# Loading the first x tile ahead of a small weight, and rearranging the other start-up loads, in a two-layer attention and GLU kernel

## The chip, the cores and the metric

The kernel runs on one core of one Trainium2 chip. The metric is device time in microseconds (us). The granted TensorE clock, where it is on record, is 0.999 to 1.00 in all but four executions, where it is 0.996. Before the change: 391.91 us, median of 3 runs (391.82 to 392.07).

## The reference

Two linear-attention blocks alternate with two gated MLP blocks over x of shape 1 x 2048 x 512 in bf16. Cut to what matters here:

```python
def _A_ref(x, wqkv, w_phi, wo):               # 32 heads of 16
    q, k, v = split(x @ wqkv)
    pq, pk = q @ w_phi, k @ w_phi             # per head, 16 x 16
    phi_q = concat(softmax(pq), softmax(-pq)) # 32 features a head
    phi_k = concat(softmax(pk), softmax(-pk))
    kv, z = phi_k^T v, sum(phi_k)             # sums over all 2048 rows
    return ((phi_q kv) / (phi_q z + 1e-6)) @ wo
def _B_ref(x, W_gate, W_up, W_down):
    return (relu(x W_gate) * (x W_up)) @ W_down
x = x + _A_ref(layernorm(x)); x = x + _B_ref(layernorm(x))   # and both once more
```

`kv` sums over all rows, so no query of the first block can be finished before the keys of all 16 tiles of 128 rows are normalised and summed. I call the time up to there the first phase.

## The kernel before

The kernel records about 3,700 operations, each with an estimated duration, and a list scheduler inside the kernel file puts them in an order for each engine (SyncE's queue of DMAs included). It tries many orders and keeps the one that its own model finds shortest.

The start-up loads:

```python
dma("sp", phi_c <- A_w_phi)                       # the small weight, 16 KB in rows of 32 bytes
for ic in range(4):
    dma("act", wk_n[:, ic, :] <- A_wqkv[...])     # key weight, four pieces of 128 KB, ACT's queue
for t in range(4):
    ldx(t, t + 1)                                 # x tiles 0 to 3, 128 KB each, SyncE's queue
first = [R_wkn[3]]                                # the bulk loads wait for the fourth piece
ldx(4, 8, first)                                  # 512 KB
dma("sp", wv_p <- A_wqkv[:, 1024:1536], first)    # value weight, 512 KB
ldx(8, 12, first)
ldx(12, 16, first)
dma_start_transpose(WqT <- A_wqkv[:, 0:512])      # query weight
... # cut
for j, o in enumerate(...):
    o.boost = 1e9 - 1e7 * j                       # these keep their order in the queues
```

What the first phase does with a tile: VectorE takes statistics (`bn_stats`); for tiles 8 to 15 GpSimd turns four tiles' statistics into a mean and a factor (`agg`, `rv`, `rstd`, `nmr`: "aggregation"); VectorE or ScalarE applies them (`ytile`); the result is transposed into `yT`, by TensorE for tiles 0 to 3 and by a DMA on SyncE's queue for the others; TensorE multiplies by the key and value weights; ScalarE takes exponentials (`expk`); VectorE sums them (`Zk`) and inverts (`rZk`); GpSimd multiplies (`expk <- expk, rZk`: "normalisation"); TensorE accumulates the key-value sums, which VectorE copies into `kvbd`.

```python
self.dma_tr(... k.yT[:, :, t*128:(t+1)*128], k.ytile[:, yb, :])   # a tile's transposition, SyncE
pieces.append(... dma("sp", k.wo_p[h:128:8] <- wo_v[h]), [rd])    # output weight, eight loads, SyncE
...
for t in tiles(0):
    self.ln(t, "L0", pe_bank=(7 if t < 2 else 6), copy_act=True)
...
for i, piece in enumerate(pieces):
    piece(self.r("yT", 15 if i < 8 else 15))      # the later weights wait for tile 15, not for tile 14
```

The softmax here doesn't subtract the row's maximum and nothing guards it: scores larger than these inputs give would overflow.

## Time and profile before

| what | before | read from |
|---|---|---|
| span of the profiled run | 390.3 us | head of the page |
| VectorE's first statistics | 4.32 us | timeline |
| gate opens, tiles 4 to 7 land | 6.23 us, 10.51 us | chain of waits |
| tiles 8 to 11 land | 13.42 us | semaphore records of the trace |
| aggregation of tiles 8 to 11 starts | 17.42 us | chain of waits |
| last normalisation ends | 52.00 us | timeline of GpSimd |

A landing time, here and below, is the moment when all 16 completions of a load had reached its semaphore. Where the chain of waits shows a load, it ends at this moment.

From the page of the kernel before, the head, the row of TensorE (busy time and share of the span, instructions) and the chain of waits by engine:

```profile
span 390.3 us, 6397 instructions
...
PE 379.4 (97%) x2331; PEld 208.0 (53%) x2331; DVE 272.0 (70%) x547; ACT 206.6 (53%) x389; POOL 168.5 (43%) x284
...
PE 88%; POOL 4%; ACT 3%; DMA 2%; DVE 1%; issue 1%; ACTq 0%; POOLq 0%
```

In the first phase it is not the only one. The table of windows of the kernel before has, for each stretch, its length, each engine's busy time with its number of instructions, the granted clock, the mean busy share of the DMA engines and their GB/s:

```profile
0.00:10.00 10.00, 5.41 (x41) 3.87 (x42) 5.01 (x14) 5.13 (x9) 5.52 (x22) 1.00 0.64 184
10.00:20.00 10.00, 9.05 (x50) 4.50 (x49) 9.42 (x21) 8.88 (x18) 4.60 (x14) 1.00 0.88 223
40.00:50.00 10.00, 10.00 (x88) 6.09 (x86) 10.00 (x13) 7.70 (x14) 10.00 (x6) 1.00 0.71 222
```

The third and fifth busy times are VectorE and GpSimd: from 10 us on VectorE hardly pauses, and from 20 us on GpSimd neither. TensorE (the first) looks full in the last of these stretches too, but matmuls overlap (at 66.01 us eight of 0.38 us each take 1.73 us) and their ends are modelled. The chain of waits of the kernel before (start, duration, what) shows how the phase begins:

```profile
2.22 4.01 DMA hT<-in_A_wqkv_dram
...
6.25 4.26 DMA x_sb<-in_A_x_dram
...
10.53 2.47 DVE stats L551 x4
...
15.55 1.80 DVE stats L551 x3
...
17.42 0.20 POOL agg L570
```

The fourth key piece opens the gate, tiles 4 to 7 follow, then come statistics, then aggregation. GpSimd's timeline of the kernel before (start, duration, line, operation) shows how the phase ends, with fourteen operations in a row up to 52.00:

```profile
21.07 1.93 POOL L634 TENSOR_TENSOR expk<-expk,rZk 128x1024 bf16<-128x1024 bf16 x1
...
24.21 1.93 POOL L634 TENSOR_TENSOR expk<-expk,rZk 128x1024 bf16<-128x1024 bf16 x1
...
26.25 25.75 POOL L634 TENSOR_TENSOR expk<-expk,rZk 128x1024 bf16<-128x1024 bf16 x14
```

SyncE's queue of the kernel before near 38 us will matter later. Three of the eight output-weight loads stand ahead of the last tile's transposition:

```profile
36.03 2.41 SPq L537 DMA_DIRECT2D wo_p<-in_A_wo_dram  x3
38.48 1.27 SPq L597 DMA_TRANSPOSE yT<-ytile  x1
39.80 3.14 SPq L537 DMA_DIRECT2D wo_p<-in_A_wo_dram  x5
```

The DMA rate behind the gate, again as windows of the kernel before (last column GB/s), stays above 340 from 9 to 12 us:

```profile
9.00:10.00 1.00, 1.00 (x8) 0.58 (x7) 0.78 (x3) 1.00 (x3) 0.57 (x1) 1.00 1.09 385
10.00:11.00 1.00, 1.00 (x8) 0.72 (x7) 0.57 (x2) 0.83 (x3) 0.00 (x0) 1.00 1.02 341
11.00:12.00 1.00, 0.50 (x6) 0.21 (x3) 1.00 (x3) 0.95 (x3) 0.00 (x0) 1.00 1.03 352
```

### The profile page before, as it was taken

To read this page: it belongs to the slowest core of one execution; us is meant where nothing else is said; L and a number is where in the kernel's file an instruction comes from. 1 tells how busy PE (TensorE), PEld (TensorE's weight loads), DVE (VectorE), ACT (ScalarE), POOL (GpSimd) and SP (SyncE) were. 2 spreads that over 40 slices of the span, in tenths; PEclk is the share of its full clock that TensorE was granted. 3 is DMA by queue.
4 is the path that set the end of the run, shared out by engine and by line. 5 is a ranking of instruction groups with operands and counts; after the bars stand their busy time and mean duration, and the time that the engine had idled before them with its cause. 6 is when DMAs were issued, how large, how long until landed. Compare 5 with 4: busy or idle time off the path is not lost.

```text
span 390.3 us, 6397 instructions
## 1 busy us (share of the span) xinstructions
PE 379.4 (97%) x2331; PEld 208.0 (53%) x2331; DVE 272.0 (70%) x547; ACT 206.6 (53%) x389; POOL 168.5 (43%) x284
## 2 busy tenths in 40 slices
PE   5999989999999999999999999999999999999997
PEld 3445554667644544444444457567774554444444
DVE  4999978877766888866766777897986776232222
ACT  5898859834633404533453484985563462553340
POOL 5499936641724363372244543584553242100000
DMA  6833682311311322401000110132323132100002
GB/s 179 228 67 71 191 299 53 69 40 32 53 40 27 43 55 44 84 10 28 14 15 0 27 29 3 40 80 57 55 55 69 27 42 67 29 14 27 17 12 67
DMA packets 61663, 23.01 MB, mean 59 GB/s; under 512 B 53472, under 2 KB 60608, under 8 KB 61632
## 3 DMA queue, kind: packets, MB, share of 16 engines
q1 hardware_dynamic: 60912, 22.02, 24.4%
q10 hardware_dynamic: 720, 0.59, 0.5%
q8 instruction: 18, 0.29, 0.3%
q14 instruction: 13, 0.11, 0.1%
HBM read 7.91 MB, written 2.10 MB: 26 GB/s over the span
## 4 chain that ended last, share of the span: by engine, by line
PE 88%; POOL 4%; ACT 3%; DMA 2%; DVE 1%; issue 1%; ACTq 0%; POOLq 0%
PE ps L758 39%; PE ps L785 19%; PE ps L617 7%; PE ps L737 7%; PE ps L690 6%; PE ps L706 4%; PE ps L663 3%; PE ps L648 2%; POOL expk L634 2%; ACT expq L693 2%; DVE stats L551 1%; DMA x_sb<-in_A_x_dram 1%; DMA hT<-in_A_wqkv_dram 1%; ACT expk L620 1%; POOL rstd L576 1%
## 5 line engine op out<-in xcount | busy, mean ns | idle before, releaser
L758 PE MATMUL ps<-yT,Wg 128*128 128x512 bf16 (+3 forms) x440 | 130.1, 337 | 0.5 <-DMA yT<-ytile 0.2
L758 PE MATMUL ps<-yT,Wu 128*128 128x512 bf16 (+3 forms) x440 | 129.6, 336 | 0.0
L760 ACT ACTIVATE gate_sb<-ps 128x512 bf16<-128x512 f32 (+3 forms) x110 | 55.9, 512 | 105.3 <-PE ps L758 102.9
L785 PE MATMUL ps<-Wd,hT 128*128 128x512 bf16 (+2 forms) x363 | 106.8, 373 | 0.0
L634 POOL TENSOR_TENSOR expk<-expk,rZk 128x1024 bf16<-128x1024 bf16 (+1 forms) x32 | 59.5, 1878 | 37.1 <-DVE rZk L631 19.7
L758 PEld LDWEIGHTS ps<-yT,Wg 128*128 128x128 bf16 (+1 forms) x440 | 43.4, 100 | 33.8 <-issue 1.1
L758 PEld LDWEIGHTS ps<-yT,Wu 128*128 128x128 bf16 (+1 forms) x440 | 43.7, 100 | 32.6 <-ACT expk L765 0.2
L767 DVE TENSOR_TENSOR hT<-gate_sb,expk 128x512 bf16<-128x512 bf16 (+3 forms) x73 | 29.8, 409 | 37.9 <-ACT expk L765 33.0
L785 PEld LDWEIGHTS ps<-Wd,hT 128*128 128x128 bf16 (+1 forms) x363 | 35.3, 98 | 36.6 <-DVE x_sb L787 0.6
L551 DVE BATCH_NORM_STATS2 stats<-x_sb 128x6 f32<-128x512 bf16 x64 | 42.6, 682 | 5.5 <-DMA x_sb<-in_A_x_dram 5.1
L366 ACT ACTIVATE numbf<-ps 128x432 bf16<-128x432 f32 x64 | 33.1, 536 | 19.5 <-PE ps L706 19.4
L629 DVE TENSOR_REDUCE Zk<-expk 128x64 f32<-128x1024 bf16 x32 | 37.7, 1194 | 5.7 <-ACT expk L620 5.4
L731 POOL TENSOR_TENSOR osb<-tsc 128x512 bf16<-128x512 bf16 x28 | 32.5, 1162 | 19.9 <-DVE tsc L726 17.8
L737 PE MATMUL ps<-wo_p,oT 128*128 128x512 bf16 x128 | 39.8, 379 | 0.0
L770 DVE TENSOR_TENSOR hT<-gate_sb,ps 128x512 bf16<-128x512 bf16 (+2 forms) x37 | 22.7, 613 | 20.8 <-PE ps L758 19.6
L693 ACT ACTIVATE expq<-ps 128x1024 bf16<-128x1024 f32 (+1 forms) x40 | 32.6, 861 | 7.3 <-PE ps L690 7.0
L765 ACT ACTIVATE expk<-ps 128x512 bf16<-128x512 f32 (+3 forms) x73 | 36.1, 497 | 0.1
L706 PE MATMUL ps<-kvbd,expq 128*128 128x144 bf16 x256 | 35.0, 226 | 0.5 <-ACT numbf L366 0.5
L620 ACT ACTIVATE expk<-ps 128x512 bf16<-128x512 f32 x44 | 23.9, 598 | 21.5 <-PE ps L617 21.2
L690 PE MATMUL ps<-yT,Wqp 128*128 128x512 bf16 x128 | 34.6, 379 | 0.6 <-ACT expq L693 0.5
L787 DVE TENSOR_TENSOR x_sb<-x_sb,ps 128x512 bf16<-128x512 bf16 (+1 forms) x33 | 22.0, 669 | 18.8 <-PE ps L785 18.4
L559 POOL TENSOR_TENSOR rstd<-rv,mhalf 128x1 f32<-128x1 f32 (+1 forms) x53 | 31.9, 607 | 2.9
(73 smaller groups left out, 429.2 us busy)
## 6 DMA issues: line engine op xcount, KB each, us to landing
out_dram<-x_sb SPq DMA_DIRECT2D x15, 128.0 KB, 1.7
x_sb<-in_A_x_dram SPq DMA_DIRECT2D x3, 512.0 KB, 6.2
Wu<-in_B_W_up_dram SPq DMA_DIRECT2D x4, 344.0 KB, 5.9
Wg<-in_B_W_gate_dram SPq DMA_DIRECT2D x4, 344.0 KB, 5.5
Wd<-in_B_W_down_dram SPq DMA_DIRECT2D x5, 256.0 KB, 6.9
yT<-ytile SPq DMA_TRANSPOSE x60, 2.5
hT<-in_A_wqkv_dram ACTq DMA_DIRECT2D x4, 128.0 KB, 3.1
x_sb<-in_A_x_dram SPq DMA_DIRECT2D x4, 128.0 KB, 3.7
```

Source lines behind the costliest of these rows:

```text
L366: return e.activation(out, in_, ACT.Copy) if hasattr(e, "activation") else e.tensor_copy(out, in_)
L551: op("dve", (lambda t: lambda e: e.bn_stats(k.stats6[:, t, :], k.x_sb[:, t, :]))(t), [r("x", t)], [r("st", t)], 685, f"{tag} stats {t}")
L629: op("dve", lambda e: e.tensor_reduce(k.Zk[:, zb, :], k.expk[:, t, :, :].rearrange("p s (h f) -> p (s h) f", f=16), AX.X, ALU.add), [r("ex ...
L634: op(eng, (lambda s0, s1: lambda e: e.tensor_tensor(k.expk[:, t, s0:s1, :].rearrange("p s (h f) -> p (s h) f", f=16), k.expk[:, t, s0:s1, ...
L690: op("pe", (lambda c, ic, bank: lambda e: e.matmul(k.pb[bank][:], k.Wqp[:, ic, c * 128:(c + 1) * 128], k.yT[:, ic, st * 512:(st + 1) * 512 ...
L693: op("act", (lambda c0, s, b0: lambda e: e.activation(k.expq[:, st, c0:c0 + w, s, :], k.ps[:, b0:b0 + w, :], ACT.Exp, scale=(1.0 - 2.0 * s ...
L706: op("pe", (lambda s, c, j, g0, bank: lambda e: e.matmul(k.pb[bank][:, j * GW:(j + 1) * GW], k.expq[:, st, c, s, tt * 128:(tt + 1) * 128], ...
L737: op("pe", (lambda c, bank: lambda e: e.matmul(k.pb[bank][:], k.oT[:, ob, c, :], k.wo_p[:, c, :], start=(c == 0), stop=(c == NC - 1)))(c, ...
L758: op("pe", (lambda bank, W, ic, fc, Mf: lambda e: e.matmul(k.pb[bank][0:Mf, 0:n], W[:, ic, fc * 128:fc * 128 + Mf], k.yT[:, ic, c0:c0 + n] ...
L760: op("act", (lambda Mf, gb, gs: lambda e: e.activation(k.gate_sb[0:Mf, gs, 0:n], k.pb[gb][0:Mf, 0:n], ACT.Relu))(Mf, gb, gs), [self.RP[gb] ...
L765: op("act", (lambda Mf, ub, tu: lambda e: e.activation(k.expk[0:Mf, tu, 0, 0:n], k.pb[ub][0:Mf, 0:n], ACT.Copy))(Mf, ub, tu), [self.RP[ub] ...
L785: op("pe", (lambda fc, Kf, u, c0, bank, m0, m1: lambda e: e.matmul(k.pb[bank][:, m0:m1], k.hT[0:Kf, u, c0:c0 + 128], k.Wd[0:Kf, fc, m0:m1] ...
```

## The change

The intent is to start VectorE sooner. Tile 0 is issued before the small weight; the bulk loads wait for the third weight piece instead of the fourth; tiles 4 to 7 come in two loads, so that tile 4 can be used earlier; the first four transpositions on TensorE use banks 7, 0, 1, 0 instead of 7, 7, 6, 6. Some of the scheduler's estimates for loads were changed as well; they steer the order that it finds, not the loads.

```diff
+        ldx(0, 1)
+        dma("act", ... wk piece 0 ...)
         dma("sp", ... phi_c ...)
-        for ic in range(NC):
-            dma("act", ... wk piece ic ..., 96000)
-        for t in range(4):
-            ldx(t, t + 1)
-        first = [R_wkn[3]]
-        ldx(4, 8, first)
-        dma("sp", ... wv_p ..., first, ..., 524288)
+        ... # wk pieces 1 to 3 (ACT's queue) and x tiles 1 to 3 (SyncE's), in turn; cut
+        first = [R_wkn[2]]
+        ldx(4, 6, first)
+        ldx(6, 8, first)
+        dma("sp", ... wv_p ..., first, ..., 345000)
         ldx(8, 12, first)
         ldx(12, 16, first)
-        o = dma("sp", ... WqT ..., 524288);  o.dur = 7000.0
+        o = dma("sp", ... WqT ..., 422000);  o.dur = 6400.0
...
-            self.ln(t, "L0", pe_bank=(7 if t < 2 else 6), copy_act=True)
+            self.ln(t, "L0", pe_bank=(7, 0, 1, 0)[t], copy_act=True)
```

More of the change, by code (lines that the diff above doesn't have):

```diff
@@ L473, in ldx @@
         def ldx(t0, t1, after=()):
-            dma("sp", lambda e: e.dma_start(k.x_sb[:, t0:t1, :], xv[:, t0:t1, :]), list(after), [r("x", t) for t in range(t0, t1)], 131072 * (t1 - t0) if t1 > t0 + 1 else 96000, f"dma x{t0}")
+            dma("sp", lambda e: e.dma_start(k.x_sb[:, t0:t1, :], xv[:, t0:t1, :]), list(after), [r("x", t) for t in range(t0, t1)], 96000 if t1 == t0 + 1 else (131072 if t0 < 8 else 86000) * (t1 - t0), f"dma x{t0}")
+        ldx(0, 1)
+        dma("act", (lambda ic: lambda e: e.dma_start(wk_n[:, ic, :], A_wqkv[ic * 128:(ic + 1) * 128, 512:1024]))(0), [], [R_wkn[0]], 96000, f"dma wk0")
         dma("sp", lambda e: e.dma_start(k.phi_c[:], A_w_phi.rearrange("(kc hl) d f -> (hl d) kc f", hl=8)), [], [r("phi_c")], 16384, "dma phi")
-        for ic in range(NC):
-            dma("act", (lambda ic: lambda e: e.dma_start(wk_n[:, ic, :], A_wqkv[ic * 128:(ic + 1) * 128, 512:1024]))(ic), [], [R_wkn[ic]], 96000, f"dma wk{ic}")
-        for t in range(4):
-            ldx(t, t + 1)
-        first = [R_wkn[3]]
-        ldx(4, 8, first)
-        dma("sp", lambda e: e.dma_start(k.wv_p[:], wqkv_v[:, :, 1024:1536]), first, [r("wv", ic) for ic in range(NC)], 524288, "dma wv")
+        dma("act", (lambda ic: lambda e: e.dma_start(wk_n[:, ic, :], A_wqkv[ic * 128:(ic + 1) * 128, 512:1024]))(1), [], [R_wkn[1]], 96000, f"dma wk1")
+        ldx(1, 2)
+        dma("act", (lambda ic: lambda e: e.dma_start(wk_n[:, ic, :], A_wqkv[ic * 128:(ic + 1) * 128, 512:1024]))(2), [], [R_wkn[2]], 96000, f"dma wk2")
+        ldx(2, 3)
+        dma("act", (lambda ic: lambda e: e.dma_start(wk_n[:, ic, :], A_wqkv[ic * 128:(ic + 1) * 128, 512:1024]))(3), [], [R_wkn[3]], 96000, f"dma wk3")
+        ldx(3, 4)
+        first = [R_wkn[2]]
+        ldx(4, 6, first)
+        ldx(6, 8, first)
+        dma("sp", lambda e: e.dma_start(k.wv_p[:], wqkv_v[:, :, 1024:1536]), first, [r("wv", ic) for ic in range(NC)], 345000, "dma wv")
         ldx(8, 12, first)
         ldx(12, 16, first)
-        o = dma("sp", lambda e: e.dma_start_transpose(WqT, A_wqkv[:, 0:512]), first, R_WqT, 524288, "dma wqT")
-        o.dur = 7000.0
+        o = dma("sp", lambda e: e.dma_start_transpose(WqT, A_wqkv[:, 0:512]), first, R_WqT, 422000, "dma wqT")
+        o.dur = 6400.0
         for j, o in enumerate(self.prog.ops[n0:]):
```

## The prediction

> **What bounds the kernel now.** The table of windows shows TensorE busy for all but 1.2 us between 60 and 380 us, at a granted clock of 1.00, and the chain of waits is 88% TensorE. So work after about 60 us can only be shifted. The change acts in the first 52 us, which have other limits:
>
> - To 10.5 us: arrivals. The chain starts with weight piece 3 (landed 6.25), which releases the load of tiles 4 to 7 (6.25 to 10.53 for 512 KB), which releases the statistics of tile 4 on VectorE. VectorE starts at 4.32, when x tile 0 lands.
> - 10.5 to 52 us: the timeline shows VectorE busy from 10.53 to 51 and GpSimd from 17.42 (statistics of tiles 8 to 11 done) to 52.00: two aggregations of 2.6 us, fourteen normalisations of 1.93 us and two halves, 34.6 us without a pause. Then the key-value sums end and TensorE takes over.
>
> **What the change does.** No compute instruction is added or removed (the built programs have equal counts); one DMA issue of 0.43 us is added.
>
> 1. Tile 0 is issued at 0.79 instead of 1.31: landing at about 3.5 to 3.8. The small weight comes 0.5 us later; its product (GpSimd, 3.44 to 4.48) is first needed at 5.87, so this is free.
> 2. The gate moves from piece 3 (6.25) to piece 2 (used at 5.45): bulk loads start about 0.8 us earlier.
> 3. Tile 4 needs 256 KB, not 512 KB. At the 230 GB/s of this stretch (the page's second slice) 256 KB is 1.1 us. I expect tile 4 at 8.6 to 9.3, tiles 6 and 7 by 10. The Trainium skill ("Perfetto Trace Analysis", DMA Optimizations) says that splitting DMAs may let the overall task complete sooner if the DMA engines are generally idle; here they are 64% busy in the first 10 us and 88% in the next, so only order improves: later loads come at most 0.8 us earlier.
> 4. Banks 7, 0, 1, 0 instead of 7, 7, 6, 6 take away a TensorE wait (1.0 us at 12.45, on ScalarE's copy) that is not on the chain.
>
> The new order puts all sixteen statistics before the first key sum on VectorE, and both aggregations before fourteen normalisations in a row on GpSimd.
>
> **On the critical path.** VectorE's gaps between 4.3 and 10.5 (about 1.0 us) plus its earlier start can be won: 1.5 us at most. With tile 4's statistics at 9.2, aggregation starts at about 16.1; I allow 0.3 us of new gaps. The last normalisation should end at about 51.0 instead of 52.0, and that 1.0 us passes to the end. The scheduler also reorders TensorE afterwards: plus or minus 0.7 us, with slightly less waiting at the switch (50 to 62 us).
>
> **Prediction.** 390.6 us, range 389.2 to 392.0. Faster by over 2%: 0.01; within 2%: 0.98; slower by over 2%: 0.01.
>
> **What the profile would show.** Right: first statistics before 4.0; tile 4's before 9.5; aggregation at about 16; normalisations in one run ending at about 51; the same TensorE work, shifted by 1 us. Wrong: tile 4 still after 10 (the split gains nothing); or GpSimd idles before a first normalisation past 22.5 and ends at 52 again; or the gain is lost at 52 to 62 or at the second layer's switch (245 to 262).
>
> **What would make it wrong.** Earlier bulk loads delay weight piece 3 and x tile 3, which share the DMA engines; or the reordering costs or saves more on TensorE than the start does.

## The result, and the profile after

The changed kernel takes 395.35 us (median of 6 runs, 395.26 to 396.86), against 391.87 us of the kernel before (6 runs). The ratio is 1.0098, with a 95% interval of 1.0082 to 1.0115. Ratios here are the mean time of one kernel's runs over that of the other's runs of the same rounds, so they are not quite the ratio of the quoted medians. The change made the kernel about 1% slower. The predicted range ended at 392.0.

| what | before | after |
|---|---|---|
| span of the profiled run | 390.3 | 393.6 |
| VectorE's first statistics | 4.32 | 3.64 |
| third and fourth weight piece land | 5.06, 6.23 | 6.48, 7.16 |
| first bulk load issued | 6.25 | 6.49 |
| statistics of tile 4 | 10.53 | 9.31 |
| tiles 8 to 11 land | 13.42 | 14.98 |
| aggregation of tiles 8 to 11 starts | 17.42 | 18.21 |
| last normalisation ends | 52.00 | 54.01 |
| first copy into kvbd, first block | 52.52 | 54.53 |
| first copy into kvbd, second block | 238.70 | 241.58 |

The two kvbd rows cut the span into three parts. The first phase lost 2.0 us, the stretch from 52 us to the second block's sums lost 0.9 us more (187.1 instead of 186.2 us), and the rest 0.4 us (152.0 instead of 151.6 us). The last difference may be chance: in three profiles of one and the same program (e10 and e16 below) this part took 151.5, 151.7 and 152.4 us.

The same lines of the changed kernel's page:

```profile
span 393.6 us, 6346 instructions
...
PE 377.2 (96%) x2288; PEld 208.1 (53%) x2331; DVE 268.1 (68%) x547; ACT 207.7 (53%) x389; POOL 169.1 (43%) x284
...
PE 84%; DVE 5%; DMA 4%; issue 4%; ACT 1%; SPq 0%; ACTq 0%; POOL 0%; DVEq 0%; POOLq 0%
```

TensorE's busy time fell by 2.2 us although the kernel is slower. That is no gain: 43 matmul records are missing from this trace (2,288 of 2,331), while the weight loads are complete and equal (2,331 and 208 us in both). The Trainium skill ("Perfetto Trace Analysis", Identifying the Most-Contended Engine) warns for another reason, the overlap of matmuls, that their busy time is a poor measure of how close TensorE is to its limit, and advises to look at the share of peak arithmetic reached (MFU) and the busy share of LDWEIGHTS; this pair of traces agrees with the second advice. What did change is the chain: VectorE and DMA have taken 9% of it, against 3% before.

The same windows of the changed kernel:

```profile
0.00:10.00 10.00, 5.03 (x41) 3.81 (x42) 4.96 (x13) 4.63 (x8) 5.07 (x20) 1.00 0.62 165
10.00:20.00 10.00, 8.18 (x39) 3.60 (x40) 7.41 (x19) 7.92 (x15) 4.58 (x15) 1.00 0.90 219
40.00:50.00 10.00, 8.18 (x61) 4.63 (x61) 8.09 (x11) 7.09 (x11) 10.00 (x6) 1.00 0.72 202
```

VectorE has two new holes, of 2 us each, one in 10 to 20 us and one in 40 to 50 us. VectorE's timeline of the changed kernel names what ended each (in brackets: the idle time before, and the releaser):

```profile
9.31 2.47 DVE L556 BATCH_NORM_STATS2 stats<-x_sb 128x6 f32<-128x512 bf16 x4
...
15.01 1.29 DVE L556 BATCH_NORM_STATS2 stats<-x_sb 128x6 f32<-128x512 bf16 x2 [2.59 <-DMA x_sb<-in_A_x_dram]
...
47.43 1.22 DVE L634 TENSOR_REDUCE Zk<-expk 128x64 f32<-128x1024 bf16 x1 [1.84 <-ACT expk L625]
```

Tile 4 did come 1.2 us earlier, as intended; but VectorE then ran out of tiles and waited 2.59 us for tile 8. The chain of waits of the changed kernel follows both holes back:

```profile
1.73 4.75 DMA hT<-in_A_wqkv_dram
...
7.95 7.04 DMA x_sb<-in_A_x_dram
...
41.90 3.29 DMA yT<-ytile
...
45.24 1.04 PE ps L622 x4
```

The load of tiles 8 to 11 was issued at 7.95 and took 7.04 us. The second hole starts at a tile's transposition that SyncE issued only at 41.90. SyncE's queue of the changed kernel shows why:

```profile
36.64 5.22 SPq L542 DMA_DIRECT2D wo_p<-in_A_wo_dram  x7
41.90 1.27 SPq L602 DMA_TRANSPOSE yT<-ytile  x1
43.22 0.59 SPq L542 DMA_DIRECT2D wo_p<-in_A_wo_dram  x1
```

The scheduler put seven output-weight loads, not three, ahead of tile 14's transposition. They take SyncE 5.2 us. Tile 14's values were ready at 38.88, so the transposition stood 3.0 us behind loads that nobody needed yet, and TensorE waited 1.77 us for it. The timelines of VectorE and of TensorE in the changed kernel:

```profile
38.10 0.78 DVE L597 TENSOR_SCALAR ytile<-x_sb,rstd,nmr 128x512 bf16<-128x512 bf16 x1
...
45.24 1.04 PE L622 MATMUL ps<-Wkp,yT 128*128 128x512 bf16 x4 [1.77 <-DMA yT<-ytile]
```

So ScalarE's exponentials and VectorE's sums came late, and GpSimd's run broke before its last operation. GpSimd's timeline of the changed kernel:

```profile
23.45 28.13 POOL L639 TENSOR_TENSOR expk<-expk,rZk 128x1024 bf16<-128x1024 bf16 x15
52.51 1.50 POOL L639 TENSOR_TENSOR expk<-expk,rZk 128x512 bf16<-128x512 bf16 x1 [0.94 <-DVE rZk L636]
```

The DMA rate behind the gate, windows of the changed kernel, has a hole where the kernel before moved 340 to 385 GB/s:

```profile
9.00:10.00 1.00, 1.00 (x11) 0.72 (x10) 1.00 (x4) 1.00 (x3) 0.74 (x2) 1.00 0.81 211
10.00:11.00 1.00, 1.00 (x4) 0.40 (x4) 1.00 (x2) 0.89 (x2) 0.00 (x0) 1.00 0.79 186
11.00:12.00 1.00, 1.00 (x5) 0.34 (x3) 1.00 (x7) 0.11 (x1) 0.00 (x0) 1.00 0.81 261
```

So two theories stand against each other. Theory A: the new order that the scheduler found costs the time. Theory B: the loads themselves arrive worse and cost it.

### The profile page after: what moved, and what is told of

Same layout as the page of the kernel before. It is cut to its first block, busy times and chain, and to the rows that moved or that the text cites. A ratio compares the mean times of both kernels' runs of the same rounds, so it can differ in the third digit from the quotient of the medians. Undisturbed runs are those within 1.5% of the kernel's fastest.

```text
span 393.6 us, 6346 instructions
## 1 busy us (share of the span) xinstructions
PE 377.2 (96%) x2288; PEld 208.1 (53%) x2331; DVE 268.1 (68%) x547; ACT 207.7 (53%) x389; POOL 169.1 (43%) x284
## 4 chain that ended last, share of the span: by engine, by line
PE 84%; DVE 5%; DMA 4%; issue 4%; ACT 1%; SPq 0%; ACTq 0%; POOL 0%; DVEq 0%; POOLq 0%
PE ps L763 39%; PE ps L790 19%; PE ps L622 8%; PE ps L742 6%; PE ps L695 6%; PE ps L711 4%; PE ps L668 3%; DMA x_sb<-in_A_x_dram 2%; DVE rZk L636 1%; DMA yT<-ytile 1%; DVE stats L556 1%; DMA hT<-in_A_wqkv_dram 1%; DVE Zk L634 1%; DVE ytile L599 0%; ACT expq L698 0%
## 5 line engine op out<-in xcount | busy, mean ns | idle before, releaser
L763 PE MATMUL ps<-yT,Wg 128*128 128x512 bf16 (+3 forms) x436 | 125.9, 336 | 1.4 <-ACT expk L770 0.7
L763 PE MATMUL ps<-yT,Wu 128*128 128x512 bf16 (+3 forms) x435 | 123.8, 336 | 0.4
L790 PE MATMUL ps<-Wd,hT 128*128 128x512 bf16 (+2 forms) x351 | 104.4, 372 | 0.6
L772 DVE TENSOR_TENSOR hT<-gate_sb,expk 128x512 bf16<-128x512 bf16 (+3 forms) x73 | 28.9, 396 | 31.3 <-ACT expk L770 30.6
L742 PE MATMUL ps<-wo_p,oT 128*128 128x512 bf16 x122 | 38.1, 379 | 0.7 <-DMA oT<-osb 0.5
L563 POOL TENSOR_SCALAR rv<-mv 128x1 f32<-128x1 f32 (+1 forms) x53 | 12.7, 244 | 56.8 <-DVE mv L558 56.7
L711 PE MATMUL ps<-kvbd,expq 128*128 128x144 bf16 x256 | 34.1, 226 | 0.5 <-ACT numbf L366 0.4
L695 PE MATMUL ps<-yT,Wqp 128*128 128x512 bf16 x121 | 32.8, 379 | 0.8 <-ACT expq L698 0.5
```

Source lines behind the costliest of these rows:

```text
L695: op("pe", (lambda c, ic, bank: lambda e: e.matmul(k.pb[bank][:], k.Wqp[:, ic, c * 128:(c + 1) * 128], k.yT[:, ic, st * 512:(st + 1) * 512 ...
L711: op("pe", (lambda s, c, j, g0, bank: lambda e: e.matmul(k.pb[bank][:, j * GW:(j + 1) * GW], k.expq[:, st, c, s, tt * 128:(tt + 1) * 128], ...
L742: op("pe", (lambda c, bank: lambda e: e.matmul(k.pb[bank][:], k.oT[:, ob, c, :], k.wo_p[:, c, :], start=(c == 0), stop=(c == NC - 1)))(c, ...
L763: op("pe", (lambda bank, W, ic, fc, Mf: lambda e: e.matmul(k.pb[bank][0:Mf, 0:n], W[:, ic, fc * 128:fc * 128 + Mf], k.yT[:, ic, c0:c0 + n] ...
L790: op("pe", (lambda fc, Kf, u, c0, bank, m0, m1: lambda e: e.matmul(k.pb[bank][:, m0:m1], k.hT[0:Kf, u, c0:c0 + 128], k.Wd[0:Kf, fc, m0:m1] ...
```

## The experiments

To tell them apart, the loads and the order had to be varied separately. Every kernel from e1 to e12, and e16, emits the wanted loads but takes its order, operation by operation, from the scheduler's answer for another variant:

```diff
-            prog.schedule()
-            prog.prepare()
+            self.prog.schedule()                    # of the variant whose order is wanted
+            rank = {key: o.start for o, key in self.prog.keyed()}
+            ...                                     # emit the wanted variant anew
+            prog.follow(rank)                       # topological order, smallest rank first
+            prog.prepare()                          # waits are derived anew, as always
```

Replaying a kernel's own order in this way gives back its instructions and waits without a difference (compared, not run). In e1 to e9 and e12 every compute engine has exactly the order of the kernel named. All kernels gave correct results. No kernel for the banks alone was run (the number e7 is left out), so the banks have no verdict of their own. The new banks are in e1 to e3, e8 to e11 and e16, the old ones in e4 to e6 and e12. So "order" below always includes the banks where the order is new. e1, which has them and everything else of the change in the old order, is 0.18% slower, so they hardly cost more than that there, unless another part of the change made up for them.

The results, with the kernel before on the same chip. "Norm." is the end of the last normalisation, "8-11" the landing of tiles 8 to 11, both of the one profiled execution.

| run | loads | order | us (median) | before, same chip | ratio (95%) | norm. | 8-11 |
|---|---|---|---|---|---|---|---|
| before | old | old | 391.87 | | | 52.00 | 13.42 |
| changed | new | new | 395.35 | 391.87 | 1.0098 (1.0082-1.0115) | 54.01 | 14.98 |
| e1 | new | old | 393.10 | 392.30 | 1.0018 (0.9995-1.0040) | 52.50 | 14.99 |
| e2 | old | new | 394.46 | 392.30 | 1.0052 (1.0028-1.0076) | 52.55 | 13.04 |
| e3 | new | new, tile 14 first | 394.86 | 392.30 | 1.0064 (1.0035-1.0094) | 52.77 | 14.72 |
| e4 | tile 0 first | old | 392.37 | 392.30 | 1.0004 (0.9979-1.0029) | 51.97 | 14.49 |
| e5 | gate on piece 3 | old | 391.96 | 391.41 | 1.0009 (0.9995-1.0024) | 51.88 | 13.05 |
| e6 | split | old | 391.79 | 391.41 | 1.0007 (0.9993-1.0022) | 51.72 | 14.21 |
| e8 | new, unsplit | new | 394.41 | 391.41 | 1.0082 (1.0063-1.0101) | 52.47 | 13.46 |
| e9 | old | new, tile 14 first | 393.12 | 391.41 | 1.0038 (1.0020-1.0055) | 51.28 | 13.22 |
| e10 | old | new start, old rest | 392.35 | 391.97 | 1.0017 (0.9992-1.0041) | 51.32 | 13.28 |
| e11 | gate, weight behind | as e10 | 392.64 | 391.97 | 1.0010 (0.9996-1.0024) | 52.15 | 10.44 |
| e12 | tiles 8-11 split | old | 392.06 | 391.97 | 1.0001 (0.9987-1.0015) | 52.23 | 12.46 and 13.21 |
| e13 | new | jittered | 394.16 | 391.97 | 1.0054 (1.0041-1.0068) | 53.68 | 15.31 |
| e14 | old | jittered | 393.36 | 391.83 | 1.0045 (1.0028-1.0062) | 51.77 | 13.97 |
| e15 | old | jittered | 393.51 | 391.83 | 1.0046 (1.0030-1.0063) | 51.89 | 13.54 |

Differences of under about 0.7 us are not settled by these times: executions of one kernel on these chips scatter by 0.5 to 3 us.

### e1: the whole change in the old order

```diff
+ loads, gate, split and banks of the changed kernel
+ order of the kernel before on every compute engine
```

> The whole change (loads, gate, split, banks), but every compute engine keeps the order of instructions of the kernel before. Theory A (the new order that the scheduler made costs the time): about 391.0 us, at most 391.8, because the same loads then cost nothing. Theory B (the loads themselves arrive worse: third weight piece at 6.5 us, tiles 8 to 11 at 15.0 us, and VectorE idles): about 394 us, with VectorE waiting over 1.5 us for tiles 8 to 11.

Measured: ratio 1.0018, about 0.8 us at the medians, between the two expectations. The loads do arrive worse (tiles 8 to 11 at 14.99), but VectorE waits only 0.48 us for them, because in the old order a key sum (`Zk` of tile 0, 1.2 us) stands between the statistics of tile 7 and those of tile 8. Theory B's wait of over 1.5 us did not come. In this order the loads cost 0.18% of the 0.98% that the whole change costs, with an interval from nothing to 0.40%.

### e2: the old loads in the new order

```diff
+ loads, gate and single load of tiles 4 to 7 of the kernel before
+ order and banks of the changed kernel
```

> The loads and the gate of the kernel before, but the order of instructions of the changed kernel on every compute engine (and its banks, which that order needs). Theory A: about 395 us, like the changed kernel, with the 1.8 us wait of TensorE for the transposed tile near 45 us still there. Theory B: about 391.5 us.

Measured: ratio 1.0052, 2.2 us at the medians. Again between the two, nearer to theory A. The wait of TensorE for tile 14's transposition is still there without any of the new loads (TensorE's timeline of this run):

```profile
43.55 1.04 PE L672 MATMUL ps<-Wkp,yT 128*128 128x512 bf16 x4 [1.54 <-DMA yT<-ytile]
```

So the order costs about 2 us by itself, and the loads another 1.5 to 2 on top of it, though they cost only about 0.8 us in the old order (none of these differences of two ratios is known to better than about 1 us). Both theories hold in part, and the parts do not simply add.

### e3: the changed kernel with tile 14 ahead of the output weight

```diff
+ rank["L0 tr 14"] = rank["L0 apply 14"] + 0.1
+ rank["dma wo0".."dma wo7"] = max(own rank, rank["L0 apply 14"] + 0.2)
```

> The changed kernel with one move on SyncE's queue: the transposition of tile 14 stands ahead of the eight loads of the output weight, and not behind seven of them. If that place is the main part of the loss: the wait of 1.8 us at 45 us goes, the normalisations end at about 52.5 in place of 54.0, and the time is about 393.3 us (2 us less than the changed kernel). If the loads at the start are the cause: the wait goes or becomes another, and the time stays at 395 within 0.4 us.

Measured: ratio 1.0064 against 1.0098 of the changed kernel, so about 1.3 us less; 2 us had been expected. GpSimd's run is whole again and ends at 52.77 (timeline of this run):

```profile
23.18 29.58 POOL L694 TENSOR_TENSOR expk<-expk,rZk 128x1024 bf16<-128x1024 bf16 x16
```

It still starts at 23.18, since tiles 8 to 11 landed at 14.72. The first phase ends 1.24 us earlier here than in the changed kernel (54.01 to 52.77), and with the old loads 1.27 us earlier (e2 to e9: 52.55 to 51.28). Not all of that is the place of the transposition: GpSimd's first normalisation starts 0.27 and 0.31 us earlier in these two pairs, at 22 to 23 us, long before tile 14's turn in the queue, so this part has another cause (in the first pair tiles 8 to 11 landed 0.26 us earlier). From there to the last normalisation it is 30.56 us with tile 14 behind seven loads (changed kernel, e2) and 29.58 and 29.59 us with it in front (e3, e9). So the place costs 0.97 us. The Trainium skill ("DMA: Bandwidth & Descriptors", Anatomy of one DMA), in a section on DMAs that GpSimd issues, says of the DMA engines that they do not wait on semaphores: the wait happens on the issuing sequencer, before dispatch. No run here tests that, but this trace shows that time spent issuing is spent there too: the ready transposition went out only when SyncE had got through the seven loads ahead of it.

### e4, e5, e6: single edits in the old order

```diff
e4:  + ldx(0, 1) ahead of the load of phi_c; gate on piece 4
e5:  - first = [R_wkn[3]]
     + first = [R_wkn[2]]
e6:  - ldx(4, 8, first)
     + ldx(4, 6, first); ldx(6, 8, first)
```

> The kernel before with one part of the change: x tile 0 is issued ahead of the small weight; order, gate and loads are otherwise as before. If putting tile 0 first is what delays the other early pieces: the third weight piece is used by TensorE at about 6.5 us (5.45 before), the fourth lands after 7 us (6.23 before), the bulk loads start 0.8 us later, and the time is about 392.7 us. If the order of these two loads is harmless: 391.9 within 0.3 us.

> The kernel before with one part of the change: the bulk loads wait for the third weight piece and not for the fourth; small weight first, tiles 4 to 7 in one load, old order. If the gate by itself does what was predicted of it: the third piece lands near 5.1 us, tiles 4 to 7 at about 9.4 us (10.5 before), aggregation on GpSimd starts at about 16.4 (17.4), normalisations end at about 51.0 (52.0), and the time is 0.7 to 1.0 us below the kernel before run beside it. If earlier bulk loads only take bandwidth from the pieces they pass: pieces 4 of the weight and tile 3 land later by 0.5 us or more, and the time is the same within 0.3 us.

> The kernel before with one part of the change: tiles 4 to 7 in two loads; everything else as before. If the split is what slows the loads behind it: tiles 4 and 5 at about 9.3 us, but the value weight lands near 13.4 us (11.9 before) and tiles 8 to 11 near 14.8 us (13.4 before), and the time rises by 0.3 to 0.8 us. If the split is harmless and the late landings come from tile 0 ahead or from the gate: value weight near 12, tiles 8 to 11 near 13.5 us, and the time is equal or up to 0.5 us lower.

None of the three changes the time by an amount that these runs settle (ratios 1.0004, 1.0009, 1.0007); all three expectations of a lasting gain or loss missed. Their landings are telling all the same:

- e4: with tile 0 first, the third and fourth pieces landed at 6.33 and 6.98 (before: 5.06 and 6.23), and the bulk loads started at 7.00. The expected delay of the loads is there, but the expected loss of 0.8 us is not: the normalisations end at 51.97.
- e5: the gate opened at 5.74, half a microsecond earlier than in the kernel before (0.60 us before the fourth piece of the same execution, at 6.34), and tiles 4 to 7 landed at 9.17 instead of 10.51. But the aggregation started at 17.29, against 17.42. The gain stopped at VectorE: its next item in this order is the key sum of tile 0, and it waited 0.42 us for ScalarE's exponentials (the sum began at 13.28, before: 13.20).
- e6: tiles 4 and 5 landed at 8.37, but the value weight at 12.76 and tiles 8 to 11 at 14.21, from a gate that had opened at 5.75. That is 8.46 us after the gate; in the kernel before it was 7.17 us.

The edits also cancel. With tile 0 first and the gate on piece 3 the first bulk load was issued at 6.49, 6.26, 6.13, 6.10 and 6.18 us (changed kernel, e1, e3, e8, e13); with the small weight first and the gate on piece 4, at 5.7 to 6.5 us in nine runs, 6.25 in the kernel before. The gate moved by one piece, and so did the pieces. The delay by tile 0 is clear of the scatter: over all profiles the third and fourth pieces landed at 4.82 to 5.87 and 5.67 to 6.47 us with the small weight first (twelve), and at 6.08 to 6.48 and 6.73 to 7.16 us with tile 0 first (six).

### e8: the changed kernel, unsplit

```diff
- ldx(4, 6, first); ldx(6, 8, first)
+ ldx(4, 8, first)
```

> The changed kernel with tiles 4 to 7 in one load again; tile 0 first, gate on the third piece and the new order stay. If the split delays the loads behind it: tiles 8 to 11 land at about 13.7 us (15.0 in the changed kernel), the transposition of tile 14 starts about 1.2 us earlier, and the time is about 1.2 us below the changed kernel, so about 2.2 us above the kernel before. If tile 0 first is the cause: tiles 8 to 11 still near 14.8 us and the time within 0.4 us of the changed kernel (3.3 us above before).

Tiles 8 to 11 landed at 13.46 instead of 14.98 and the normalisations ended at 52.47 instead of 54.01, as expected of a harmful split. The time fell less than the first phase did: ratio 1.0082, 0.6 us below the changed kernel's ratio, where 1.2 us had been expected; the two intervals overlap. The two slowest of its six executions (395.77 and 395.13 us) are those with a granted clock of 0.996; the other four average 394.30 us, a ratio of about 1.0070 to the kernel before. That would be the expected gain, but it was not a comparison planned beforehand. Windows of this run (last column GB/s) show a shorter hole, one slice of 208 GB/s, where the changed kernel had 211, 186 and 261:

```profile
9.00:10.00 1.00, 0.82 (x9) 0.51 (x7) 0.40 (x1) 1.00 (x4) 0.39 (x1) 1.00 1.06 367
10.00:11.00 1.00, 1.00 (x6) 0.33 (x5) 1.00 (x3) 0.85 (x3) 0.00 (x0) 1.00 0.68 208
```

Over all runs with the value weight between and tiles 8 to 11 in one load, these landed 6.8 to 7.9 us after the first bulk issue in the eleven profiles without the split, and 8.5 to 9.1 us after it in the five with it (changed kernel, e1, e3, e6, e13). That the split delays what follows is shown; why it does so is not.

### e9: the new order with both losses of its first phase taken out

```diff
+ loads of the kernel before
+ order of the changed kernel, tile 14's transposition first as in e3
```

> The new order with both suspected losses of its first phase taken out: the loads of the kernel before, and the transposition of tile 14 ahead of the output weight on SyncE's queue. If these two are the whole loss of the first phase: normalisations end at about 51.7 us (52.0 before, 54.0 in the changed kernel). What is then left against the kernel before, expected 0.6 to 1.2 us, belongs to the order of TensorE's later work, after 60 us. If the new order were as good as the old one after 60 us, the time would be equal to the kernel before or up to 0.5 us less.

The first phase ended at 51.28, which is 0.72 us earlier than in the kernel before. That is the best of four profiles of this start with the old loads (e9, e10 and e16: 51.28, 51.32, 51.67 and 52.20, on average 0.4 us earlier). And the gain did not reach the end: the profiled span is 390.4 against 390.3, and the timed ratio is 1.0038, about 1.5 us slower (the profiled execution was the fastest of its six).

Where it went can be read from the first copies into kvbd of the two blocks. The stretch between them took 186.18 to 186.20 us in all six profiles with the old order (before, e1, e4, e5, e6, e12) and 187.05 to 187.19 us in all five with the new one (changed kernel, e2, e3, e8, e9), whatever the loads. So 0.9 us of the loss after 52 us belongs to the new order; which of its waits make it up is open.

### e10: new order for the first phase, old order for the rest

```diff
+ rank of the changed kernel's order up to the first kvbd copies, of the old order afterwards
+ loads of the kernel before, tile 14 first
```

> The loads of the kernel before, the new order for the work up to the end of the first key-value sums (with the transposition of tile 14 ahead of the output weight), and the old order for everything after. If the gain of the first phase seen with these loads and this order (0.7 us) is lost only through the later order: normalisations end at about 51.3 us (52.0 before) and the time is about 0.6 us below the kernel before. If such a gain is swallowed after 60 us whatever the order: within 0.3 us of the kernel before.

The expected gain of 0.6 us is not in the times (ratio 1.0017, interval on both sides of 1), though the profiled span is 390.0. Part of the first phase's gain went at the seam of the two orders: the stretch between the two blocks' first copies into kvbd is 186.64 us here, 0.45 more than in the old order. Single executions ran from 391.25 to 394.37 us. The two slowest (394.37 and 393.89) had a granted clock of 0.996, as in e8; the other four average 391.9 us, against 392.0 of the kernel before. Whether the clock made these two slow was not tested. Two more profiles of the same kernel were taken.

### e16: the same kernel again, twice

> The same kernel as e10_new_start_old_rest, for one more profile. If the spread of its times comes from the landing of tiles 8 to 11: time and end of the normalisations move together (an execution at 393 us shows normalisations ending about 1 to 2 us later, at 52 to 53 us, and tiles 8 to 11 landing after 14 us). If it comes from later: the normalisations end at 51.3 us in a slow execution too.

> The same kernel as e10_new_start_old_rest once more, and the same two readings: either the end of the normalisations moves with the time and with the landing of tiles 8 to 11, or it stays at 51.3 us whatever the time.

VectorE's timeline, the statistics of tile 4 and those of tile 8, first in e10 (391.69 us):

```profile
9.49 2.47 DVE L622 BATCH_NORM_STATS2 stats<-x_sb 128x6 f32<-128x512 bf16 x4 [0.54 <-DMA x_sb<-in_A_x_dram]
...
13.30 1.29 DVE L622 BATCH_NORM_STATS2 stats<-x_sb 128x6 f32<-128x512 bf16 x2 [0.69 <-DMA x_sb<-in_A_x_dram]
```

and then in e16_again_a (392.75 us):

```profile
10.37 2.47 DVE L622 BATCH_NORM_STATS2 stats<-x_sb 128x6 f32<-128x512 bf16 x4 [1.33 <-DMA x_sb<-in_A_x_dram]
...
14.10 1.29 DVE L622 BATCH_NORM_STATS2 stats<-x_sb 128x6 f32<-128x512 bf16 x2 [0.62 <-DMA x_sb<-in_A_x_dram]
```

The same program got its tiles 0.8 to 0.9 us later, and its normalisations ended at 52.20 instead of 51.32. In e16_again_b tiles 8 to 11 landed at 13.46 and the normalisations ended at 51.67; this run lost a further 0.8 us at 264 us, where TensorE waited for an attention output's transposition. Across the runs of the new start with a free queue, landing and end move together: 13.22 to 51.28 (e9), 13.28 to 51.32, 13.46 to 51.67, 14.08 to 52.20, 14.72 to 52.77 (e3). In the old order they do not up to 14.5: landings of 13.05, 13.42, 14.21 and 14.49 gave ends of 51.88, 52.00, 51.72 and 51.97. Only the latest landing, 14.99 in e1, shows, with 52.50 (e12, with its split load, is at 13.21 and 52.23). So the new order has spent slack that the old order had against late tiles, and gives its gain back when they are late. The executions with late times in e10's own series were not profiled, so how much of that scatter is of this kind is open.

### e11: tiles 8 to 11 ahead of the value weight

```diff
- first = [R_wkn[3]]
+ first = [R_wkn[2]]
  ldx(4, 8, first)
- dma("sp", ... wv_p ..., first)
  ldx(8, 12, first)
+ dma("sp", ... wv_p ..., first)
```

> As the run before it, and the loads reordered for what VectorE waits for: gate on the third piece, small weight first, tiles 4 to 7 in one load, then tiles 8 to 11 ahead of the value weight. If the landing of tiles 8 to 11 limits the new order: they land at about 11.5 us, VectorE waits less than 0.2 us for them, aggregation starts at about 15.7 us, normalisations end at about 50.5, and the time is 1.2 to 1.6 us below the kernel before. Rival: the value weight, now landing near 13 us, holds up TensorE and through it the key sums; then the normalisations end no earlier than 51.3 and the time equals the run before it.

This was an attempt at a version that beats both, and the rival won. Tiles 8 to 11 landed at 10.44 and the aggregation started at 16.06, but the value weight landed at 12.87 and held up TensorE (timeline of this run):

```profile
12.92 1.90 PE L688 MATMUL ps<-wv_p,yT 128*128 128x512 bf16 x8 [1.37 <-DMA wv_p<-in_A_wqkv_dram]
```

Later VectorE waited for exponentials, GpSimd for VectorE, and the normalisations ended at 52.15. The ratio is 1.0010, the same as before. With about 3.7 MB to load first (an estimate from the sizes in the source), moving one load ahead moves another back.

### e12: the split on tiles 8 to 11 instead

```diff
- ldx(8, 12, first)
+ ldx(8, 10, first); ldx(10, 12, first)
```

> The kernel before with tiles 8 to 11 in two loads, in place of tiles 4 to 7 as in the change. If two half loads in a row delay whatever comes behind them: value weight at about 12 us as before, tiles 10 and 11 at 13.5, and the load of tiles 12 to 15 lands over 1 us later than the 14.9 us of the kernel before. If only the place right behind the gate is sensitive: tiles 12 to 15 at about 14.9 and the transposed weight at 16.6 us, as before. Time within 0.5 us of the kernel before in either case.

The value weight landed at 11.14, tiles 10 and 11 at 13.21, and tiles 12 to 15 at 14.63, against 14.86 before. So two half loads do not in general delay what stands behind them; right behind the gate they did, in five profiles of five. (e12 is a single profile.)

### e13, e14, e15: other orders by chance

```diff
+ jitter = random.Random(seed)
+ for o in ops:
+     o.dur *= jitter.uniform(0.99, 1.01)    # the scheduler's estimates only
```

e13 has the changed kernel's code, e14 and e15 the code of the kernel before, each scheduled anew.

> The changed kernel with its scheduler's estimates of every duration multiplied by random factors between 0.99 and 1.01, which gives another order of all engines; the loads and what they wait for stay. Here two loads of the output weight, not seven, stand ahead of the last transposition. If the time is made by which order the scheduler happened to find: it differs from the changed kernel by over 1 us, about 1.5 us less (the place of the transposition), so near 1.5 us above the kernel before. If it is made by the loads: still 3 us or more above the kernel before.

> The kernel before, its loads untouched, with the scheduler's estimates of durations multiplied by random factors between 0.99 and 1.01: another order on every engine. If the order by itself is worth microseconds: the time differs from the kernel before by more than 0.8 us, more likely upwards since the kernel before was kept as the best of its kind. If only the loads matter: within 0.5 us of the kernel before.

> As the run before it with another seed; in this order the transposition of tile 14 stands ahead of all eight loads of the output weight. If that place is what decides: first phase ends at 52 us or earlier and the time is within 0.5 us of the kernel before. If the later order decides as well: up to 1.5 us above, with the first phase at 52 us.

Other orders with the untouched old loads are 1.0045 and 1.0046, about 1.6 us slower, though their first phases end at 51.77 and 51.89, no later than before: the loss is after 52 us (second-block sums at 239.46 in e14, against 238.70; the stretch behind them 152.9 us in e15, against 151.6). The jittered order with the new loads is 1.0054, so 1.7 us better than the changed kernel. In these three runs a change of 1% in estimates moved the time by about 1.6 us, up or down, without any change to what the kernel computes or loads.

## Why the prediction was wrong

The step that failed first: "bulk loads start about 0.8 us earlier", and with it "only order improves: later loads come at most 0.8 us earlier". The bulk loads started 0.24 us later, and tiles 8 to 11 came 1.56 us later, mostly because of the split (e6, e8). From this "aggregation starts at about 16.1" fell (18.21) and with it "the last normalisation should end at about 51.0" (54.01). The second failure is a term of the sum that was mis-sized: reordering was put at "plus or minus 0.7 us" for TensorE and at nothing for SyncE. It cost 0.97 us at SyncE's queue and 0.9 us between 52 us and the second block's sums.

Point by point:

- Tile 0 earlier: right. First statistics at 3.64. But tile 0 first also pushed the third and fourth weight pieces back, by 0.6 to 1.4 us and 0.6 to 0.9 us (e4 and the changed kernel against e5 and the kernel before); the prediction named such a delay only as a risk, and blamed the bulk loads for it.
- Small weight later, "this is free": not quite. TensorE waited 0.7 us for its product in the changed kernel. It is not on the chain.
- The gate 0.8 us earlier: wrong. It opened 0.24 us later, because the piece that it waits for came later. The gate alone does open earlier (e5, 0.5 us), and even then the old order turned 1.3 us of earlier tiles into 0.1 us of aggregation.
- Tile 4 at 8.6 to 9.3: right (landed 9.20). The skill's advice on splitting ("Perfetto Trace Analysis", DMA Optimizations) was read in the prediction as harmless at worst; here the half load did start sooner, and the loads behind came 1.3 us later (e6). The advice is for DMA engines that are generally idle, and the prediction itself had noted that these were not.
- Banks: the TensorE wait at 12.45 went, and 0.9 us of waiting for the value weight came in its place. The banks alone were not run (e1 has them in the old order, with little loss).
- VectorE's gaps "can be won": wrong. The gap moved from in front of tile 4 to in front of tile 8 and grew to 2.59 us.
- Reordering: mis-sized. The list of the new order, at hand before the prediction, showed seven output-weight loads ahead of the last transposition (three before), and this was overlooked. It is worth 0.97 us of the first phase. After 52 us the changed kernel lost 0.9 us more by its order, which no single wait explains; TensorE's small new pauses make up part of it, and the remainder is not located. The last 0.4 us are within the scatter. The prediction did name as a risk that "the reordering costs or saves more on TensorE than the start does".

The first phase of the profiled runs can be added up. Its end is the start of GpSimd's first normalisation plus the length of GpSimd's run from there, and this length follows the order, whatever the loads (except in e11, where the late value weight held up TensorE: 30.85):

| profiles | first normalisation | run to the last one |
|---|---|---|
| old order (before, e1, e4, e5, e6, e12) | 20.77 to 21.55 | 30.93 to 30.95 |
| new order, tiles 4 to 7 in one load (e2, e8) | 21.92, 22.00 | 30.55, 30.56 |
| new start, tile 14 first, one load (e9, e10, e16) | 21.69 to 22.62 | 29.57 to 29.59 |
| new order, split load (changed, e3) | 23.45, 23.18 | 30.56, 29.58 |

The new order does both aggregations before the run, where the old one does part of the second within it: it starts about 0.9 us later and then needs 1.35 us less. The place of tile 14 takes back 0.97 us of that. The split puts the start off by a further 1.3 us on average (e8, with all new loads but the split, starts as early as with the old ones). The changed kernel, against the kernel before: 2.38 us lost at the start, 0.37 us won in the run, together 2.0.

By the timed ratios, which are the firmer measure of the whole, old loads in the new order cost 0.52% and the new loads in that order another 0.46%. Counted the other way, the new loads in the old order cost 0.18% (e1) and the new order on top of them 0.80%. So there is no one share of each: the loads cost as much as they do only because the new order lost the slack against them. Counted either way, the order's part is no smaller than that of the loads, within what these intervals can tell. The share of the split in the timed result (0.16% by the ratios, with overlapping intervals, and about 0.28% without the two executions at 0.996) is less certain than its share in the first phase.

No version tried is faster than the kernel before. None of the other orders that were scheduled or composed beat its order with certainty.

## What to carry to other kernels

Where a scheduler inside the kernel decides the order, separate the two things that an edit does: replay the old order with the new code, and the new order with the old code, before explaining any time. Read the new order of the DMA queues as closely as that of the engines; a transposition behind a few loads that are not yet needed cost as much here (0.97 us) as the tuned loads were predicted to gain (1.0 us). And an earlier arrival is worth only what the consumer's next wait leaves of it: ask which item comes after, and when that one arrives.

## What the Trainium skill lacked or had wrong

- "Perfetto Trace Analysis", DMA Optimizations: the advice to split DMAs, given for DMA engines that are generally idle, lacks the cost for loads queued behind. Here the engines of the kernel before were 64% busy in its first 10 us and 88% in the next, and tiles 8 to 11 landed 8.5 to 9.1 us after the first bulk issue with tiles 4 to 7 split (five profiles), and 6.8 to 7.9 us without (eleven); a split two places further back cost nothing (e12).
- "DMA: Bandwidth & Descriptors", Anatomy of one DMA: neither it nor another page gives a time, measured on this chip, for which one issue holds SyncE's queue in such a mixed stream. Seven 64 KB loads held SyncE for 5.2 us, and a transposition ready for 3.0 us stood behind them.
- No page has this: the landing of identical start-up loads varies by 0.8 us between executions of one program (13.28, 13.46 and 14.08 us for tiles 8 to 11 in e10 and its two repeats), which an order without slack hands on to the end of the phase.
- "Perfetto Trace Analysis": it does not say that a count of matmul records can fall short in a trace (43 of 2,331 are missing here) while the LDWEIGHTS records are complete.
